# Three small unread transfers ahead of SyncE's first loads in a sparse-attention and spectral-mix kernel

## The chip, the cores and the metric

The kernel runs on one core of one Trainium2 chip. The metric is the device time of one execution in microseconds (us), as the median of several runs. Beside it stands one profiled execution, taken by the hardware profiler, whose span runs from its first to its last instruction. All times in the steps below are counted from the start of that span.

## The reference

Two blocks follow each other. The first is attention over 8 batches, 8 heads, 576 positions and a head size of 64; heads 0 to 3 see only the last 32 positions, heads 4 to 7 only positions that are a multiple of 32 away. The second turns the result along the sequence into frequencies, multiplies the lowest 64 modes by complex matrices of 512 x 512, one for each mode, turns it back, adds, and ends in a product with `w_ch`.

```python
def _attn_ref(q, k, v):                      # q, k, v: (8, 8, 576, 64) float32
    scores = scale * np.matmul(q, k.transpose(0, 1, 3, 2))
    rel = pos[:, None] - pos[None, :]
    mask_local = (rel >= 0) & (rel < 32)
    mask_strided = (rel >= 0) & (pos[None, :] % 32 == pos[:, None] % 32)
    scores = np.where(masks, scores, -1000000000.0)   # heads 0-3 local, 4-7 strided
    attn = softmax(scores)
    return np.matmul(attn, v)

def _moe_ref(x, w_r, w_i, w_ch):             # x: (8, 576, 512); w_r, w_i: (64, 512, 512)
    X = np.fft.rfft(x, axis=1)
    Xr, Xi = np.real(X[:, :64]), np.imag(X[:, :64])
    Yr = np.einsum('bmd,mde->bme', Xr, w_r) - np.einsum('bmd,mde->bme', Xi, w_i)
    Yi = np.einsum('bmd,mde->bme', Xr, w_i) + np.einsum('bmd,mde->bme', Xi, w_r)
    u = x + np.fft.irfft(Y, n=576, axis=1)   # Y is Yr + 1j*Yi in the lowest 64 modes
    return u + np.maximum(u @ w_ch, 0.0)
```

Inputs and output are float32. By far the largest inputs are `w_r` and `w_i`, 64 matrices of 1 MB each.

## The kernel before

The order of the work is written out by hand: each engine runs its instructions in the order of the program, and the framework only adds the semaphore waits.

The kernel has four stages. First, strided attention (heads 4 to 7), batch by batch, until about 80 us; the helpers are `str_v`, `str_q`, `str_k` (transposes on TensorE, copies on VectorE and ScalarE), `str_scores` and `str_values`. Second, local attention (heads 0 to 3), batch by batch, mixed with the first of the modes. Third, the rest of the modes: each mode's two matrices come as one tile `wt` and are multiplied at line 597 or 630 as soon as they have landed. Last, the inverse transform, the product with `w_ch`, and the output, from `osb` tiles by SyncE (line 1028, and at the very end line 1031 by SyncE and ScalarE).

Loading goes by three queues. GpSimd issues everything that is converted from float32 to 16 bits on the way: the rows of v, q and k into the tile `ring` (`load_str`, lines 218 to 222, and `load_loc`) and the weights into `wt` (`w_fetch`, lines 182 to 190). In the profile this is queue q0. A row is 2048 elements, so it appears as one packet of 4 KB. GpSimd's transfers use eight semaphores in turn, so each of them waits for the landing of the eighth transfer before it. A weight transfer also waits until the tile that it overwrites has been used.

The constants are 16-bit tables of the program: `cT` (the Fourier table), `cM6`, `cM5` and `cMl` (the masks) and `cI` (the identity that transposes need). `const_load` (line 109) loads them as they are. ScalarE issues `cI`, `cM6` and `cM5` (queue q10), SyncE `cT` and `cMl` (queue q1). Their issues are among the first instructions of these engines.

The start of the program is this, at line 765:

```python
    psum_pools(tp=3, sc=3, av=2)
    load_str(0, 1)                              # GpSimd: v, q, k of batch 0
    const_load(nc.scalar, "cI", "cM6", "cM5")
    load_str(1, 1)                              # GpSimd: v, q, k of batch 1
    const_load(nc.sync, "cT", "cMl")
    strided_tokens()                            # GpSimd: L327, L328, then L329 reads cT
    load_str(2, 2)                              # GpSimd: v, q, k of batches 2 and 3
    w_fetch()
```

For each of v, q and k in this order, `load_str(0, 1)` issues 64 rows of its batch (line 220) and then eight rows of each of two batches (line 222). `strided_tokens` copies `cT` into `PL` in another order, so GpSimd must have `cT` before it issues the loads of batches 2 and 3. TensorE's first work is the transposes of v at line 276 (`str_v`), which need the rows of v and `cI`. After its two constants SyncE issues nothing until the outputs.

Of the kernel before, what the change touches and what calls it, by code (L numbers as in the profile page):

```python
# [10 lines left out]
FP = mybir.dt.float32  # L11
# [45 lines left out]
def kernel(  # L57
# [10 lines left out]
    nc = tc.nc  # L68
    PSUM = bass.MemoryType.PSUM
    ctx.enter_context(tc.manual_schedule())  # L70
    consts = ctx.enter_context(tc.tile_pool(name="consts", bufs=1))
# [6 lines left out]
    def psum_pools(**bufs):  # L78
        pctx.close()
        pss.clear()  # L80
        for n, c in bufs.items():
            pss[n] = pctx.enter_context(
                tc.tile_pool(name="ps_" + n, bufs=c, space=PSUM)
            )
# [22 lines left out]
    def const_load(eng, *which):  # L107
        for n in which:
            eng.dma_start(cs[n][:, 0 : hosts[names.index(n)].shape[1]], drams[n])
# [100 lines left out]
    def load_str(b, nb):  # L210
        for vi in (2, 0, 1):
            n = 3 * (b % 4) + SLOT[vi]
            two = ring[:, n : n + 4 : 3, :]
            src = SRC[vi][b - b % 2 : b - b % 2 + 2, 4:8].rearrange(
                "b h (c r) d -> (h c) b (r d)", r=32
            )
            if nb == 2:
                nc.gpsimd.dma_start(two[0:64], src[0:64])
            else:
                nc.gpsimd.dma_start(ring[0:64, n, :], src[0:64, b % 2])  # L220
            if b % 2 == 0:
                nc.gpsimd.dma_start(two[64:72], src[64:72])
# [539 lines left out]
            )  # L762


    psum_pools(tp=3, sc=3, av=2)
    load_str(0, 1)
    const_load(nc.scalar, "cI", "cM6", "cM5")
    load_str(1, 1)
    const_load(nc.sync, "cT", "cMl")
    strided_tokens()  # L770
# [342 lines left out]
```

## Time and profile before

| | |
|---|---|
| median of 3 runs | 427.93 us (427.37 to 429.17) |
| profiled execution, span | 426.7 us |
| TensorE / VectorE / ScalarE / GpSimd busy | 81% / 55% / 51% / 26% of the span |
| bytes by DMA | 91.62 MB, mean 215 GB/s |
| share of queue q0 (GpSimd) of the 16 DMA engines | 96.2% |
| first DMA issue, on SyncE and on ScalarE | 0.74 us |
| first DMA issue on GpSimd | 1.23 us |
| `cT` / `cMl`, issue to landing | 2.4 / 2.3 us |
| TensorE's first instruction | 7.1 us |
| first output issued | 396.88 us |

The profiled execution's own time is its span; the median of the unprofiled runs is 1.2 us longer. Bytes are counted as they are written: a row that is converted counts 4 KB, though 8 KB are read. The view by windows gives for each stretch the busy time of each engine, the clock that TensorE was granted, and at the end the busy share of the DMA engines (above 1 where packets overlap) and the rate. The DMA view gives the packets that began in the stretch, the megabytes, and the share of 16 engines' time for each queue. Packets of a few bytes close a transfer; they count in the number of packets and hardly in the time. The chain of waits gives the start, the length and the work of each piece.

### The profile page before, as it was taken

How to read it: one execution, taken by the hardware profiler on the slowest of the kernel's cores; microseconds unless marked ns; L12 is line 12 of the kernel's file. 1: busy time of each engine (PE TensorE's matmuls, PEld its weight loads, DVE VectorE, ACT ScalarE, POOL GpSimd, SP SyncE). 2: the span in 40 equal slices, each digit the busy share in tenths (PEclk: the TensorE clock that was granted, in tenths of full speed). 3: DMA queues.
4: the chain of work that ended last, by engine and by line, in shares of the span. 5: the costliest groups of instructions: out<-in, count | busy, mean ns of one | idle time of the engine just before them, and what ended most of it. 6: DMA issues, size and time to landing. Idle time of an engine off the chain costs nothing.

```text
span 426.7 us, 9768 instructions
## 1 busy us (share of the span) xinstructions
PE 346.4 (81%) x4167; PEld 208.2 (49%) x4167; DVE 234.7 (55%) x466; ACT 218.3 (51%) x390; POOL 110.7 (26%) x196
## 2 busy tenths in 40 slices
PE   2977878769999698889768788878788867889993
PEld 2866767554656365566433344435444423445330
DVE  3788778851355154356113246746676354655884
ACT  1687678643656356556642235423442444443872
POOL 8332333322423222222222322222232222210000
PEclk9999899967999689999995889989999979989997
DMA  8999999999999999999999999999999999995698
GB/s 150 210 212 212 213 213 213 211 211 211 214 213 213 213 213 215 212 214 215 210 214 211 213 214 213 210 213 215 212 213 214 213 213 214 214 212 105 244 355 287
DMA packets 30938, 91.62 MB, mean 215 GB/s; under 512 B 4464, under 2 KB 5232, under 8 KB 30896
## 3 DMA queue, kind: packets, MB, share of 16 engines
q0 software_dynamic: 25168, 81.28, 96.2%
q1 hardware_dynamic: 4976, 9.13, 5.9%
q10 hardware_dynamic: 752, 0.61, 0.5%
q8 instruction: 32, 0.52, 0.5%
q14 instruction: 10, 0.08, 0.0%
HBM read 162.83 MB, written 9.44 MB: 404 GB/s over the span
## 4 chain that ended last, share of the span: by engine, by line
DMA 47%; PE 29%; DVE 14%; ACT 5%; issue 3%; DVEq 0%; POOL 0%; ACTq 0%; POOLq 0%
DMA wt<-in_moe_w_i_dram 38%; DMA wt<-in_moe_w_r_dram 7%; PE y L597 5%; DVE xb L241 3%; DVE kz L283 3%; PE p L987 2%; ACT X L251 2%; PE sc L532 2%; PE tp L413 2%; PE sc L459 1%; PE p L1001 1%; PE y L532 1%; PE p L760 1%; DVE yy L752 1%; DVE rec L240 1%
## 5 line engine op out<-in xcount | busy, mean ns | idle before, releaser
L597 PE MATMUL y<-wt,X 128*32 128x512 f16 (+1 forms) x448 | 70.9, 430 | 20.1 <-DMA wt<-in_moe_w_i_dram 20.1
L186 POOL DMA_DIRECT2D wt<-in_moe_w_r_dram x59 | 34.7, 588 | 126.4 <-PE y L597 56.3
L186 POOL DMA_DIRECT2D wt<-in_moe_w_i_dram x60 | 35.4, 590 | 68.3 <-DMA wt<-in_moe_w_i_dram 44.4
L597 PEld LDWEIGHTS <-X 128*32 128x32 f16 (+1 forms) x448 | 28.1, 140 | 39.4 <-DMA wt<-in_moe_w_i_dram 18.6
L727 DVE COPY xo<-tp 128x512 f16<-128x512 f16 x32 | 22.1, 691 | 36.8 <-PE tp L725 36.8
L726 ACT ACTIVATE v<-sc 128x512 f16<-128x512 f32 x32 | 19.1, 597 | 44.2 <-PE sc L717 44.2
L717 PE MATMUL sc<-w_cp,xT 128*128 128x512 f16 x128 | 36.9, 410 | 1.9 <-DVE xT L690 1.9
L489 ACT ACTIVATE PL<-sc 128x480 f16<-128x480 f32 (+1 forms) x48 | 27.0, 578 | 21.3 <-PE sc L475 21.0
L241 DVE TENSOR_TENSOR xb<-av,rec 90x256 f16<-90x256 f32 (+2 forms) x80 | 36.0, 450 | 2.8
L240 DVE RECIPROCAL rec<-av 90x4 f32<-90x4 f32 (+2 forms) x80 | 14.6, 183 | 39.3 <-PE av L504 28.2
L251 ACT ACTIVATE yr<-y 128x512 f16<-128x512 f32 x28 | 16.7, 597 | 36.8 <-PE y L597 35.6
L961 DVE TENSOR_TENSOR xo<-p,xo 128x1024 f16<-128x1024 f32 x16 | 19.6, 1225 | 21.7 <-PE p L760 21.7
L420 DVE COPY qT<-tp 128x576 f16<-128x576 f16 x16 | 11.9, 752 | 34.7 <-PE tp L413 34.7
L251 ACT ACTIVATE v<-p 128x1024 f16<-128x1024 f32 x16 | 16.4, 1023 | 23.1 <-PE p L760 23.1
L378 ACT ACTIVATE PL<-sc 90x360 f16<-90x360 f32 (+1 forms) x48 | 22.7, 490 | 7.0 <-PE sc L371 6.4
L251 ACT ACTIVATE v<-tp 128x640 f16<-128x640 f16 (+1 forms) x24 | 19.0, 807 | 11.8 <-PE tp L447 9.3
L413 PE MATMUL tp<-cI_s,ring 64*64 64x64 f16 x864 | 22.4, 197 | 2.7 <-DVE qT L420 2.4
L459 PE MATMUL sc<-cMl_s,cI_s 128*128 128x480 f16 (+1 forms) x48 | 19.4, 405 | 4.5 <-ACT PL L489 2.9
L276 PE MATMUL tp<-cI_s,ring 72*128 72x72 f16 x256 | 15.4, 207 | 8.7 <-DMA ring<-in_v_dram 7.1
L413 PEld LDWEIGHTS <-ring 64*64 64x64 f16 x864 | 17.5, 110 | 9.4 <-issue 5.4
L251 ACT ACTIVATE kz<-tp 64x360 f16<-64x360 f16 (+1 forms) x32 | 18.9, 592 | 6.2 <-PE tp L413 5.2
L1013 ACT ACTIVATE rl<-p 128x1024 f32<-128x1024 f32 (+1 forms) x19 | 18.4, 979 | 5.7 <-PE p L1001 3.1
(142 smaller groups left out, 737.9 us busy)
## 6 DMA issues: line engine op xcount, KB each, us to landing
wt<-in_moe_w_i_dram POOLq DMA_DIRECT2D x60, 512.0 KB, 18.8
wt<-in_moe_w_r_dram POOLq DMA_DIRECT2D x59, 512.0 KB, 17.7
out_dram<-osb SPq DMA_DIRECT2D x15, 512.0 KB, 3.4
ring<-in_v_dram POOLq DMA_DIRECT2D x8, 288.0 KB, 13.4
ring<-in_q_dram POOLq DMA_DIRECT2D x8, 288.0 KB, 13.6
ring<-in_k_dram POOLq DMA_DIRECT2D x8, 288.0 KB, 13.1
ring<-in_v_dram POOLq DMA_DIRECT2D x3, 512.0 KB, 14.8
ring<-in_q_dram POOLq DMA_DIRECT2D x3, 512.0 KB, 14.8
```

Of the source, the lines that this page charges most:

```text
L186: nc.gpsimd.dma_start(dst, rows)
L241: nc.vector.tensor_tensor(out=dst, in0=val.rearrange("p h (q c) -> p h c q", c=4), in1=rec[0:n, 0:pieces] .to_broadcast((n, pieces, 64)) . ...
L251: nc.scalar.activation(out=out, in_=in_, func=ACTF.Copy)
L378: nc.scalar.activation(out=PS[0:n, ds(POFF[t], 4 * n)], in_=scp[0:n, 0 : 4 * n], func=ACTF.Exp, scale=SCALE,)
L413: nc.tensor.transpose(tp[ds(64 * hp, 64), ds(64 * i, 64)], qn[ds(64 * hp, 64), ds(64 * (9 * g + i), 64)], idn[ds(64 * hp, 64), ds(64 * hp, ...
L459: nc.tensor.matmul(scp[:, 0 : n * times].rearrange("p (h x) -> p h x", h=times), idn, mask_rows("cMl", n, times), start=True, stop=False,)
L489: nc.scalar.activation(out=dst, in_=src, func=ACTF.Exp, scale=SCALE)
L597: nc.tensor.matmul(yp[ds(a, 32), :], Xh[half][pr, c].rearrange("p b r (h m) -> p (b r h) m", h=2)[:, :, mm % 32], wt[pr, XC[c], :], start= ...
L717: nc.tensor.matmul(vp, xT[:, ch], w_chs["cp"][:, ch, :], start=(ch == 0), stop=(ch == 3),)
L726: nc.scalar.activation(out=v0, in_=vp, func=ACTF.Copy)
L727: nc.vector.tensor_copy(out=xo.rearrange("p (h q c) -> p h q c", h=2, c=4), in_=tp[:, 0:512].rearrange("p (h c q) -> p h q c", h=2, c=4),)
L961: nc.vector.tensor_tensor(out=xo, in0=up[:, 0:n], in1=xo, op=AluOp.add)
```

## The change

A tile `seen` of 16 partitions with three rows of 16 float32 values (192 bytes per partition) is added to the pool of constants. A helper `touch` loads into one of its rows a corner of an input: batch 0, head 4, the first 16 positions and the first 16 of the 64 values, so 16 rows of 64 bytes. It is called three times on SyncE: for v, then for q, then for k. Nothing reads `seen`.

```diff
+    seen = consts.tile([16, 3, 16], FP, name="seen")
+
+    def touch(eng, i, src):
+        eng.dma_start(seen[:, i], src[0, 4, 0:16, 0:16])
+
     psum_pools(tp=3, sc=3, av=2)
+    touch(nc.sync, 0, v)
     load_str(0, 1)
     const_load(nc.scalar, "cI", "cM6", "cM5")
+    touch(nc.sync, 1, q)
+    touch(nc.sync, 2, k)
     load_str(1, 1)
     const_load(nc.sync, "cT", "cMl")
     strided_tokens()
```

On SyncE the order is now v's, q's and k's touch, `cT`, `cMl`, and then the outputs. On the other engines the order of the instructions is the same as before. The tile `seen` lies behind the constants, and the tiles that come after it lie 192 bytes further up in each partition.

## The prediction

> **What bounds the kernel now.** I read the page's slices first, because the change acts on the first microseconds only, and the question is whether anything gained or lost there reaches the end.
>
> ```profile
> DMA  8999999999999999999999999999999999995698
> GB/s 150 210 212 212 213 213 213 211 211 211 214 213 213 213 213 215 212 214 215 210 214 211 213 214 213 210 213 215 212 213 214 213 213 214 214 212 105 244 355 287
> q0 software_dynamic: 25168, 81.28, 96.2%
> ```
>
> The DMA engines run full from the second slice to about 384 us, at 210 to 215 GB/s in every slice, and nearly all of it is q0, the queue that GpSimd feeds with rows of v, q, k and the weights. A stage in which the engines never slacken ends when its bytes are through. So the kernel is a stream of fixed volume, then a tail of about 49 us that starts when the last weights have landed. What the start of the stream loses or gains, the end loses or gains. Only the first slice is below the rate (150 GB/s), so I cut it up by windows.
>
> ```profile
> core 0: us, PE busy (x) PEld busy (x) DVE busy (x) ACT busy (x) POOL busy (x), PEclk, DMA share, GB/s
> 0.00:1.70 1.70, 0.00 (x0) 0.00 (x0) 0.64 (x1) 0.00 (x0) 0.68 (x5) 1.00 0.00 0
> 1.70:2.80 1.10, 0.00 (x0) 0.00 (x0) 0.43 (x1) 0.69 (x1) 1.10 (x3) 1.00 0.90 227
> 2.80:4.05 1.25, 0.00 (x0) 0.00 (x0) 0.00 (x0) 0.60 (x1) 1.25 (x3) 1.00 0.86 72
> 4.05:5.06 1.01, 0.00 (x0) 0.00 (x0) 0.00 (x0) 0.00 (x0) 1.01 (x3) 1.00 0.99 178
> 5.06:7.00 1.94, 0.00 (x0) 0.00 (x0) 0.00 (x0) 0.00 (x0) 1.10 (x3) 1.00 1.09 179
> 7.00:9.00 2.00, 1.21 (x19) 1.09 (x20) 1.14 (x7) 0.83 (x2) 2.00 (x6) 1.00 1.04 193
> 9.00:16.00 7.00, 6.56 (x77) 5.88 (x77) 6.12 (x12) 3.50 (x7) 3.85 (x7) 1.00 1.06 211
> ```
>
> The last two columns count: until 1.70 nothing moves, until 2.80 the constants move, and from 2.80 to 4.05 the engines are 0.86 busy yet move 72 GB/s. The DMA view of that stretch, of its later part, and of the next ones shows who holds them:
>
> ```profile
> q0 software_dynamic: 16, 0.07, 77.2%
> ...
> q10 hardware_dynamic: 1, 0.00, 0.2%
> ...
> q0 software_dynamic: 43, 0.17, 90.3%
> ...
> q0 software_dynamic: 131, 0.33, 103.0%
> ...
> q0 software_dynamic: 151, 0.39, 104.0%
> ...
> q0 software_dynamic: 488, 1.48, 106.5%
> ```
>
> The first line is 2.80 to 4.05: 16 rows, one on each engine. The next is 3.10 to 4.05 alone; then 4.05 to 5.06, 5.06 to 7.00, 7.00 to 9.00 and 9.00 to 16.00. At the steady end, 488 packets less the 128 tiny ones that close transfers are 360 rows of 4 KB; 1.065 x 7.00 x 16 engines / 360 = 0.331 us a row. The first 16 rows, all of v, took 0.772 x 1.25 x 16 / 16 = 0.965 us each: 0.63 us more than steady, on every engine. Something at the first read of v makes the engines wait; the touches aim at that. By the same division (less tiny packets) the 42 rows after them are 0.016 us over steady, the 81 rows to 7.00 are 0.064 over, the 94 to 9.00 0.023 over: 0.04, 0.32 and 0.14 us of each engine. All waiting of this kind is 0.63 + 0.04 + 0.32 + 0.14 = 1.13 us.
>
> **The change, part by part.**
>
> *The prize.* From 2.80 to 9.00 the queue moved 16 + 42 + 81 + 94 = 233 rows, 0.954 MB. At 211 GB/s that is 4.52 us and it took 6.20: the stream is 1.68 us late. Of this 0.32 us is the constants' own transfers on q1 and q10 after 2.80 (6.5% and 2.7% of 1.25 us, 9.1% of 1.01, 5.8% of 1.94). So 1.36 us is the most that warm first reads can give back to the stream, about 0.3% of the kernel; above 1.13 us it is idleness, not waiting.
>
> *The touches' own transfers.* 16 rows of 64 bytes and a closing packet on each engine, three times: 96 packets. The ACT queue's small packets took 19.1% of 1.10 us x 16 for 202, so 0.017 us each; 96 x 0.017 / 16 = 0.10 us.
>
> *The touches' place.* SyncE issues cT at 0.74, and its packets appear with the first DMA work at about 1.70. The touch of v takes that place, 1.1 us before v's first rows at 2.80. So it is early enough: it meets the first wait instead of the rows. The wait itself does not vanish. Its length is between the mean excess of 0.63 us and what the whole stretch allows, 1.25 less one steady row, 0.92 us. It then runs from 1.70 to 2.33 or 2.62.
>
> *What it displaces.* That time was not idle: the constants fill 0.90 of 1.70 to 2.80, 0.99 us of every engine. If they must wait behind the touch, they run after it and push into the rows. The row for this is the later part of v's wait: from 3.10 to 4.05 the ACT queue moved one packet, though the second cM transfer was issued by 2.1, landed 5.5 us after its issue, and moved 44 and 99 packets on q10 in the two windows that follow. A waiting read held the engine for all queues. So I count the touch's wait as 0.63 to 0.92 us pushed into the stream.
>
> The Trainium skill says otherwise in part ("DMA: Bandwidth & Descriptors", section "Queues, rings and completion order"): each engine goes round the queues that have work, packet by packet, so a queue that waits would not stop another. The row of 3.10 to 4.05 disagrees, with one packet in 0.95 us. By the rule the constants would pass and the sum would be -1.26 us; by the row it is the sum below.
>
> *The touches of q and k.* They follow 0.4 us apart. Bound from below: their waits run while that of v runs, 0 us. From above: each holds all engines in turn, 2 x 0.63 to 2 x 0.92 us. Nearest rows: q's and k's first rows cost only 0.32 + 0.14 us in 5.06 to 9.00, and small packets at 0.017 us each are far too short for a whole read, so reads are asked for ahead of their turn. I take 0.2 us, near the lower end.
>
> *The constants of SyncE.* cT and cMl are issued three places later: an issue took 0.36 and 0.42 us, so about 1.2 us. cT landed 2.4 us after its issue, at 3.1. Late by 1.2 and by the touches' wait, 4.4 to 6 us. GpSimd wants it at 7.19 for its copy into PL (line 329), then issues the third pair of loads at 8.29. This is covered by 1 us or more; without cover GpSimd would stall, with the second batch's three loads still queued in front of the engines (16 rows per engine, about 5 us of work), so the stream would not dry up. cI goes by ACT and is needed with v at 7.12. Nothing else waits on SyncE before 396.88.
>
> *Layout.* The tile of 192 bytes moves later tiles up alike; I cost it at nothing, bounded by the run-to-run spread.
>
> Sum, main case: -1.36 + 0.78 (middle of 0.63 and 0.92) + 0.10 + 0.2 = -0.3 us. Bounds: -1.36 + 0.10 = -1.26, if the constants pass the waiting touches and nothing is pushed, and -1.36 + 3 x 0.92 + 0.10 = +1.50. The profiled execution spans 426.7 us and the runs' median is 427.93, so 1.2 us lies around it or is spread. Span 426.4, time 427.6; own range 426.7 to 429.4.
>
> **The rivals.**
>
> *Faster: the start of compute, not the stream, sets the end.* The chain of waits supports it:
>
> ```profile
> 1.23 0.66 POOL ring L220
> 1.88 5.10 DMA ring<-in_v_dram
> 6.98 0.14 issue
> 7.12 0.53 PE tp L276 x6
> ```
>
> It runs through v's landing and then through TensorE, VectorE and ScalarE for some 100 us. If v landed as a constant does (2.4 us) and every later step followed, 2.7 us would go: 425.2. Against it: a buffer freed earlier only lets GpSimd queue a transfer earlier on engines already at 212 GB/s. It needs more than 2.14 us, so nearly the whole shortening of v's landing.
>
> *Slower: the touches pay and the rows pay again.* A first-read wait may belong to the place read, and the rows lie in other places: batch 1 and other heads, while a touch reads 4 KB of batch 0, head 4. Then three waits are held in turn by all engines and nothing is spared: 3 x 0.92 + 0.10 = 2.86 us, 430.8. It decides by more than 0.5% if each touch holds the engines for over 0.68 us. Against it: rows 2 to 4 of an engine, far from the first, were within 0.016 us of steady.
>
> *No effect: the wait belongs to the GpSimd queue's first use, not to v.* Then the touches are quick, the rows wait as before, +0.1 us: 428.0. For it: the first 16 rows carry most of the excess, q's and k's far less. Against it: there is excess at q and k at all.
>
> **How the numbers follow.** The main case gets 0.50, no effect 0.13, the faster rival 0.19, the slower 0.18. The first two lie within 0.5% (2.14 us, about what a measurement of this kernel can tell from no change): same 0.63. The range starts at 425.2, the faster rival, and ends at 429.6, the main case's 429.4 and a little spread (three runs reached from 427.37 to 429.17); it leaves out the slower rival, 0.18.
>
> **What would show it.** Right: DMA work still begins near 1.7 with q1; v's first 16 q0 rows near 0.33 us each; the low GB/s found before 2.80; constants on q10 landing late; steady rate reached within 1 us of before; the last weights near 377. The copy at line 329 should wait for nothing. The faster rival shows as TensorE's first transpose about 2.7 us earlier and last weights earlier by as much. The slower one shows as q0 rows still near 0.96 us and PE's start later than 9. I am wrong altogether if the span moves by over 1.5 us with the steady rate reached when it was before.

## The result and the profile after

The change makes the kernel slower: 429.12 us in the median (427.49 to 430.88) for 427.94 before, a ratio of 1.0027 with a 95% interval of [1.0019, 1.0035]. That is a loss of 1.2 us, between 0.8 and 1.5. One of the 22 runs of before took 459.45 us, far above the others, and is left out of the ratio as a slow one. The time stays within 0.5% and within the predicted range, but it moved beyond its interval the other way than the forecast of 427.6.

The two profiled spans, 426.5 us after and 426.7 before, do not show this. The runs that list both numbers are nearly all 1.8 us longer than their spans (428.28 us for the profiled run after, with 426.5), so the profiled run before stood near 428.5, above its median, and the one after is 0.8 us below its own. What the two traces do show is the start. First the page's line of rates after:

```profile
GB/s 141 209 213 214 212 212 214 210 211 211 212 214 212 214 213 213 214 214 212 213 213 211 213 213 214 212 214 214 212 210 214 213 214 214 213 213 120 246 355 286
```

The plateau is as before, and the first slice carries 141 GB/s for 150: over a slice of 10.67 us that is 96 KB less, or 0.45 us of the stream. The view by windows after, with four of the stretches of before, shows where (last two columns: busy share of the DMA engines, GB/s):

```profile
1.70:2.80 1.10, 0.00 (x0) 0.00 (x0) 0.44 (x1) 0.67 (x1) 1.10 (x3) 1.00 0.74 101
2.80:4.05 1.25, 0.00 (x0) 0.00 (x0) 0.00 (x0) 0.61 (x1) 1.25 (x3) 1.00 0.82 145
4.05:5.06 1.01, 0.00 (x0) 0.00 (x0) 0.00 (x0) 0.00 (x0) 1.01 (x3) 1.00 0.99 207
5.06:7.00 1.94, 0.52 (x10) 0.55 (x11) 0.00 (x0) 0.00 (x0) 1.62 (x6) 1.00 0.92 137
```

From 1.70 to 2.80 the engines moved 227 GB/s before and now 101. From 2.80 to 4.05 the stream looks better than before (145 for 72 GB/s). But then, from 5.06 to 7.00, it drops to 137 GB/s for 179. The timeline of SyncE after, and the DMA issues after (size, microseconds from issue to landing):

```profile
0.74 0.40 SPq L768 DMA_DIRECT2D seen<-in_v_dram  x1
1.20 0.41 SPq L768 DMA_DIRECT2D seen<-in_q_dram  x1
1.66 0.45 SPq L768 DMA_DIRECT2D seen<-in_k_dram  x1
2.14 0.42 SPq L109 DMA_DIRECT2D cT_s<-cT  x1
2.61 0.43 SPq L109 DMA_DIRECT2D cMl_s<-cMl  x1
```

```profile
cT_s<-cT SPq DMA_DIRECT2D x1, 144.0 KB, 4.5
...
cMl_s<-cMl SPq DMA_DIRECT2D x1, 64.0 KB, 7.8
...
seen<-in_v_dram SPq DMA_DIRECT2D x1, 1.0 KB, 1.8
seen<-in_q_dram SPq DMA_DIRECT2D x1, 1.0 KB, 2.1
seen<-in_k_dram SPq DMA_DIRECT2D x1, 1.0 KB, 4.1
```

The touches of v and q land at 2.54 and 3.30. cT is issued 1.4 us later than before and lands at 6.64 instead of 3.1; cMl lands at 10.4 instead of 3.5. The DMA view after shows the exchange, first from 1.70 to 2.80, then from 5.06 to 7.00:

```profile
q0 software_dynamic: 12, 0.05, 43.6%
q10 hardware_dynamic: 282, 0.06, 26.5%
q1 hardware_dynamic: 62, 0.00, 3.5%
...
q0 software_dynamic: 54, 0.19, 73.6%
q1 hardware_dynamic: 95, 0.08, 17.9%
```

Before 2.80 the constants and touches on q1 and q10 now take 30.0% of 1.10 us, 0.33 us of every engine, where the constants took 0.99: so 0.66 us of transfers has left the stretch ahead of the rows. A part of the freed time is used, since twelve rows of v now begin before 2.80, but the constants come back among the rows: in the second stretch q0 moved 0.19 MB for 0.33 before. These are q's rows. TensorE's first work on q before, and then the chain of waits after, show what that does to it:

```profile
8.91 0.64 PE L260 MATMUL tp<-cI_s,ring 72*128 72x72 f16 x8 [0.68 <-DMA ring<-in_q_dram]
```

```profile
3.01 7.19 DMA ring<-in_q_dram
...
10.33 0.65 PE tp L260 x8
```

TensorE starts on v at 6.48, earlier than the 7.12 of before, but gets q only at 10.33 (8.91 before), and VectorE's first reciprocal comes at 18.90 for 17.48.

### The profile page after: what moved, and what is told of

It reads as the page before. It is cut to its first block, busy times and chain, and to the rows that moved or that the text cites. A ratio compares the mean times of both kernels' runs of the same rounds, so it can differ in the third digit from the quotient of the medians.

```text
span 426.5 us, 9774 instructions
## 1 busy us (share of the span) xinstructions
PE 342.9 (80%) x4167; PEld 207.5 (49%) x4167; DVE 235.0 (55%) x466; ACT 218.5 (51%) x390; POOL 111.2 (26%) x196
## 4 chain that ended last, share of the span: by engine, by line
DMA 55%; PE 23%; DVE 12%; ACT 5%; issue 3%; POOL 1%; DVEq 0%; POOLq 0%; ACTq 0%
DMA wt<-in_moe_w_i_dram 40%; DMA wt<-in_moe_w_r_dram 9%; DMA ring<-in_v_dram 4%; PE y L597 4%; DVE xb L241 3%; DVE kz L283 2%; PE p L995 2%; PE sc L532 2%; DMA ring<-in_q_dram 2%; ACT X L251 2%; PE p L1009 1%; DVE yy L752 1%; DVE rec L240 1%; PE av L392 1%; PE sc L717 1%
## 5 line engine op out<-in xcount | busy, mean ns | idle before, releaser
L597 PE MATMUL y<-wt,X 128*32 128x512 f16 (+1 forms) x448 | 68.2, 416 | 22.6 <-DMA wt<-in_moe_w_i_dram 22.6
L186 POOL DMA_DIRECT2D wt<-in_moe_w_r_dram x59 | 34.8, 590 | 121.1 <-PE y L597 40.2
L251 ACT ACTIVATE v<-p 128x1024 f16<-128x1024 f32 x16 | 16.4, 1024 | 19.7 <-PE p L760 19.7
```

The source lines that it names most:

```text
L186: nc.gpsimd.dma_start(dst, rows)
L251: nc.scalar.activation(out=out, in_=in_, func=ACTF.Copy)
L597: nc.tensor.matmul(yp[ds(a, 32), :], Xh[half][pr, c].rearrange("p b r (h m) -> p (b r h) m", h=2)[:, :, mm % 32], wt[pr, XC[c], :], start= ...
```

## The experiments

Three theories stood against each other: displaced constants (A), the first reads of v, q and k (B), and the layout (C). The first four kernels undo or isolate one part each. The measured ratios are against runs of the kernel before on the same chip, whose median was 427.90, and losses in microseconds are taken from the ratio. Edits that keep the tile or the touches of v, q and k are shown against the changed kernel, the others against the kernel before.

**Layout only.** The tile stays, the transfers go.

```diff
-    def touch(eng, i, src):
-        eng.dma_start(seen[:, i], src[0, 4, 0:16, 0:16])
+    nc.vector.memset(seen, 0.0)
...
-    touch(nc.sync, 0, v)
...
-    touch(nc.sync, 1, q)
-    touch(nc.sync, 2, k)
```

> The tile of 192 bytes is kept, so every later tile lies where it does after the change, but no transfer is made: one VectorE memset fills the tile while VectorE waits for v. Three theories for the 1.2 us that the change costs. A, displaced constants: the touches take SyncE's first places, cT and cMl come 1.4 us later and their 0.7 us of engine time falls among the rows instead of into the idle time before 2.8 us. B, first reads: reading a little of v, q and k holds the engines. C, layout: the shift of the later tiles by 192 bytes. A and B expect the time of before, 427.9 (within 0.4); C expects 429.1.

Measured: 427.98 us, ratio 1.0003 [0.9991, 1.0015]. The shift of 192 bytes costs nothing that can be measured, and the interval, up to 0.6 us, leaves out the loss of 1.2; C falls.

**The touches behind the constants.**

```diff
-    touch(nc.sync, 0, v)
...
-    touch(nc.sync, 1, q)
-    touch(nc.sync, 2, k)
...
     const_load(nc.sync, "cT", "cMl")
+    touch(nc.sync, 0, v)
+    touch(nc.sync, 1, q)
+    touch(nc.sync, 2, k)
```

> The three touches stay on SyncE but come after cT and cMl, which so have their old issue times of 0.74 and 1.16. A (displaced constants) expects the loss gone: 427.9, within 0.4, with q0's megabytes by 9 us as before. B (first reads) and C (layout) expect it kept, 429.1: the touches' reads then fall among the rows.

Measured: 428.12 us, ratio 1.0009 [1.0001, 1.0018], 0.4 us. Most of the loss goes when only the order on SyncE is put back. The small rest is above the 0.10 us that the prediction gave the touches' own packets, but its interval begins at 0.04 us.

**The same three transfers from a constant.**

```diff
+    seen = consts.tile([16, 3, 32], F16, name="seen")
...
+        eng.dma_start(seen[:, i], src[0:16, 0:32])
...
+    touch(nc.sync, 0, drams["cI"])
...
+    touch(nc.sync, 1, drams["cI"])
+    touch(nc.sync, 2, drams["cI"])
```

> The three small transfers stay in SyncE's first places with the same 16 rows of 64 bytes, but they read the program's own table cI, which is loaded anyway, and not v, q and k. A (displaced constants) expects the loss of 1.2 us as it is, 429.1, with cT landing near 6.6 and cMl near 10 as after the change. B (first reads) expects it gone, 427.9. If the touches save the rows of v some waiting, A expects slightly more than 429.1, by up to 0.3.

Measured: 428.78 us, ratio 1.0023 [1.0011, 1.0035]. That is 1.0 us: the loss is there though v, q and k are not touched. B falls.

**Late constants, no touch.**

```diff
-    const_load(nc.scalar, "cI", "cM6", "cM5")
+    const_load(nc.scalar, "cI", "cM6", "cM5", "cT", "cMl")
     load_str(1, 1)
-    const_load(nc.sync, "cT", "cMl")
```

> No touch and no tile: cT and cMl are issued by ScalarE behind its own three constants, so at about 2.1 and 2.5 us instead of 0.74 and 1.16, as late as the touches make them. A (displaced constants) expects most of the loss without any touch: 428.6 to 429.1. B and C expect the time of before, 427.9, within 0.3.

Measured: 428.57 us, ratio 1.0031 [1.0012, 1.0051]. Issuing the two constants late, on ScalarE's queue and with no touch, costs 0.7 us by the medians and 1.3 by the ratio, which two long runs (430.70 and 433.36) pull up, which is about what the change costs. The trace is that of the longest run, 433.36. The DMA view from 1.70 to 12.00 puts these kernels in two groups; the line of q0 shows packets, megabytes and share. Before, layout only, and touches last:

```profile
q0 software_dynamic: 560, 1.59, 89.0%
```

```profile
q0 software_dynamic: 570, 1.61, 88.6%
```

```profile
q0 software_dynamic: 566, 1.61, 90.0%
```

After, transfers from a constant, and late constants:

```profile
q0 software_dynamic: 529, 1.49, 83.6%
```

```profile
q0 software_dynamic: 527, 1.49, 84.7%
```

```profile
q0 software_dynamic: 544, 1.52, 84.3%
```

By 12 us the stream is 0.07 to 0.12 MB behind in the second group, which at 212 GB/s is 0.3 to 0.6 us.

**How does it reach the end: stream or compute?** The displaced constants do two things: the stream falls behind, and q lands 1.4 us late. The next kernels part them; the runs of before had a median of 427.74 there. First compute alone is made late, by repeating VectorE's first clearing.

```diff
-    nc.vector.memset(kzs[0], 0.0)
+    for _ in range(8):
+        nc.vector.memset(kzs[0], 0.0)
```

> No touch; the transfers are those of before, in the same order. VectorE clears its first tile eight times instead of once (1.07 us each), so its first copy of v starts near 9.7 instead of 7.67 and the whole start of compute is about 2 us late, which is more than the 1.4 us by which q's landing is late after the change. Two theories of how the displaced constants reach the end. A1, stream: they push the volume of the rows and weights, 0.7 us of engine time; A2, compute: they make q land later and with it every step of compute. A1 expects the time of before, 427.9, within 0.4. A2 expects 429.3 to 429.9.

Measured: 429.99 us, ratio 1.0052 [1.0034, 1.0071], just above what A2 expects. But the dose was larger than planned: each clearing was followed by 0.32 us of idleness, and the first reciprocal came at 22.24, 4.8 us late. So the same with six clearings was run, beside runs of before with a median of 427.71; the first reciprocal is at 19.45, 2.0 us late, more than the 1.4 us of the change.

> As the kernel with eight clearings of VectorE's first tile, but with six, which end near 9.1: VectorE's first copy is about 1.4 us late, as much as the change makes the first reciprocal late (18.90 for 17.48), with no transfer moved. Theory A1 (stream): the loss of the change is the stream's lag, and this kernel takes the time of before, 427.8, within 0.4. Theory A2 (compute): a start of compute that is 1.4 us late costs most of the change's 1.2 us by itself, 428.5 to 429.2, through modes that free their weight tiles too late near 100 to 120 us.

Measured: 427.75 us, ratio 0.9997 [0.9987, 1.0007]. A start of compute that is later than the change makes it shows no cost by itself; 0.3 us is the most that the interval allows. A2 in its simple form falls. The view by windows from 96 to 120 us, before, after, with six and with eight clearings, shows where the larger dose bites (last column GB/s):

```profile
96.00:120.00 24.00, 23.20 (x298) 13.06 (x296) 7.50 (x16) 12.10 (x24) 8.18 (x15) 0.89 1.09 213
```

```profile
96.00:120.00 24.00, 22.79 (x270) 12.85 (x269) 5.94 (x14) 11.66 (x24) 8.44 (x15) 0.86 1.09 212
```

```profile
96.00:120.00 24.00, 22.48 (x254) 12.53 (x255) 5.69 (x12) 11.67 (x25) 8.09 (x15) 0.83 1.08 208
```

```profile
96.00:120.00 24.00, 21.65 (x222) 12.31 (x219) 5.88 (x13) 11.87 (x24) 6.20 (x12) 0.79 0.98 187
```

With eight clearings the stream runs at 187 GB/s here: (213 - 187) x 24 us is 0.62 MB or 2.9 us; the profiled run, 430.86 us, is 3.1 above the median of before. The first modes come too late to free weight tiles: in this stretch GpSimd waited 16.4 us for the products at line 597 before it could issue weights, for 11.4 before. With six clearings the rate is 208 and the wait 13.5 us, the beginning of the same, though the time does not show it. After the change the stretch is at 212, nearly as before.

**The stream alone.** The constants are moved twice: once as before, once more among the rows, into a tile that is idle.

```diff
     const_load(nc.sync, "cT", "cMl")
+    spare = xb[7].rearrange("p a b -> p (a b)")
+    nc.sync.dma_start(spare[:, 0:576], drams["cT"])
+    nc.sync.dma_start(spare[:, 576:832], drams["cMl"])
```

> No touch; cT and cMl are loaded as before and then once more by SyncE into a tile that is idle for the first 60 us, so that 208 KB of constants (0.7 us of every engine by the rows of before) move among the rows while the first copy lands on time and nothing waits for the second. A1 (stream) expects the loss of the change without its lateness: 428.6, and up to 429.1 if the mixing of queues costs more than the engine time. A2 (compute waits for late constants or q) expects less, below 428.4, as far as q lands on time.

Measured: 428.15 us, ratio 1.0010 [1.0000, 1.0020]. That is 0.4 us, less than the 0.7 us of engine time and less than the change's 1.2; A1's 428.6 was not reached, and below 428.4 is what A2 expected. At 12 us q0 was 0.05 MB behind the kernel before (1.54 MB for 1.59). Here q's transposes also started late, at 10.26.

**Both together**, the second copy and six clearings, beside runs of before with a median of 427.80.

> The two single disturbances together and still no touch: cT and cMl moved a second time among the rows (alone +0.4 us), and compute started about 1.4 us late by six clearings on VectorE (alone -0.1 us). If the two simply add, 428.0 to 428.2. If a late stream and a late start of compute together cost more than each alone, because the first modes near 100 us then have no slack left, 428.6 to 429.1, which would account for the part of the change's loss that exceeds the engine time of the constants.

Measured: 428.63 us, ratio 1.0017 [1.0008, 1.0025], 0.7 us. The two alone add to 0.3. It points to an interaction, but the intervals overlap; this does not settle it. In its trace the stretch from 96 to 120 us ran at 213 GB/s, so it does not show the interaction there.

**Parts of the displacement.** With the touch of v alone in front (cT and cMl one place later):

> Only the touch of v stays in front; cT and cMl are one place (0.45 us) later than before instead of three. Displaced constants expects a part of the loss: cT still moves before v's first rows at 2.6 to 2.8, cMl in part behind them, 0.2 to 0.6 us, so 428.1 to 428.5. If the reads of q and k cost by themselves, it expects 427.9.

Measured: 428.02 us, ratio 1.0009 [1.0000, 1.0017], 0.4 us by the ratio, with a median just under the range expected. With the three touches between cT and cMl:

```diff
-    touch(nc.sync, 0, v)
...
+    const_load(nc.sync, "cT")
+    touch(nc.sync, 0, v)
     touch(nc.sync, 1, q)
     touch(nc.sync, 2, k)
...
-    const_load(nc.sync, "cT", "cMl")
+    const_load(nc.sync, "cMl")
```

> SyncE's order is cT, the three touches, cMl. Of the displaced constants only cMl is left, 64 KB of the 208 KB, which nothing needs before some 90 us. Displaced constants expects about a third of the loss by engine time, 0.2 to 0.5 us: 428.0 to 428.3, with q landing within 0.7 us of before. If the touches cost by coming before any rows, it expects 428.6 or more.

Measured: 428.06 us, ratio 1.0006 [0.9993, 1.0019]. Both times are near what a third of the displacement would cost, though the second cannot be told from no loss, and its q was late all the same (transposes at 10.92, for 10.33 after the change). The traces do not follow the times. From 1.70 to 12.00 the kernel with the touch of v alone moved 1.66 MB on q0, more than before, and the one with cT first moved as little as the changed kernel:

```profile
q0 software_dynamic: 528, 1.49, 86.2%
```

So how far the stream is behind at 12 us does not alone decide the loss: this kernel shows the changed kernel's lag with 0.3 us of loss, and its interval reaches from -0.3 to 0.8.

**The change again**, for a second profile.

> The changed kernel itself, beside the same runs of before, for a second profile: the first one is 0.8 us below the median of its runs. Expected 428.9 to 429.3. A1 expects the stream behind by 0.4 to 1.2 us from 16 us on and no further loss; A2 expects in a slow run an additional loss of rate between 96 and 120 us, below 211 GB/s.

Measured: 428.67 us for 427.71, ratio 1.0020 [1.0009, 1.0032]: 0.9 us, a little below the range expected and in agreement with 1.2. The first slice carried 139 GB/s, q0 had moved 1.46 MB by 12 us, and 96 to 120 us ran at 213.

**Can a touch spare the rows at all?** A single run, with the touches reading the very rows of batch 0:

```diff
+    seen = consts.tile([64, 3, 16], FP, name="seen")
...
+        rows = src[0, 4:8].rearrange("h (c r) d -> (h c) (r d)", r=32)
+        eng.dma_start(seen[:, i], rows[0:64, 0:16])
```

> The touches read the first 64 bytes of each of the 64 rows of v, q and k that batch 0 loads first, instead of 4 KB of the first row alone. It tells whether a first read can be taken from the rows at all. If the rows' waits belong to the places read, the first 64 rows of v, q and k should show no time above 0.33 us each, where v's first 16 took 0.60 after the change. If the waits come from the start of the queue and from other queues' packets on the same engine, the first rows stay near 0.6 us and q's keep their excess. The time is 429 or more in both cases, since the constants are displaced further.

Measured: 429.24 us in one run. The DMA view over the first rows of v: after from 2.50 to 3.10, transfers from a constant from 2.50 to 3.33, late constants from 2.50 to 3.20, touched rows from 2.50 to 3.15:

```profile
q0 software_dynamic: 16, 0.07, 99.8%
```

```profile
q0 software_dynamic: 16, 0.07, 69.9%
```

```profile
q0 software_dynamic: 16, 0.07, 88.4%
```

```profile
q0 software_dynamic: 17, 0.07, 89.3%
```

Share times length gives 0.60, 0.58, 0.62 and (over 17 rows) 0.55 us a row. The first rows of v take the same with touches of v, with touches of a constant, with no touch, and with touches of the same rows. They had taken 0.965 us before. That figure is not a fixed price of the constants in front either: in the seven kernels whose first constants go out as before, the same 16 rows took between 0.48 us (the second copy) and 1.12 (touches last), one trace each. That the constants' going out of the way shortened them is likely and not shown; no read ahead is seen to spare them anything.

## Why the prediction was right or wrong

**The prize: the step that failed.** The failed step is the term of -1.36 us. The prediction said that "1.36 us is the most that warm first reads can give back to the stream" and then entered all of it in the sum of the main case. Nothing of it came through a touch. The wait was read as belonging to the first read of v because it lay on v's first rows. The controls show that the 0.37 us gained there, 0.965 less 0.60, appears without any touch of v, and that the same rows can take 0.48 with the constants in place and no touch. Further back the gain was lost again: q0 moved 0.19 MB from 5.06 to 7.00 instead of 0.33. What the runs show in place of the prize is a loss, 1.0 us with touches of a constant and 0.7 to 1.3 with late constants and no touch. Without the prize the sum is 0.78 + 0.10 + 0.2, or +1.1 us, close to the measured 1.2; but that is luck, since two of its terms were reasoned otherwise than the runs show.

**What the touches displace.** The size was right, 0.63 to 0.92 us predicted and 0.66 measured as what left the time before 2.80, and the way was wrong. The engines were not held by a waiting touch: from 1.70 to 2.80 they were busy 0.74 of the time, and q10's 282 packets passed. cT was late because SyncE issued it late, three issues of 0.40 to 0.45 us, and then came behind rows. The row from 3.10 to 4.05, with one packet of q10, was read as a waiting read that holds the engines. After the change the same stretch has two packets of q1, with cT queued, while q0 moved 40 rows at 0.36 us each, near the steady 0.33. So rows in steady motion kept the constants out as well.

The rule of the Trainium skill that the prediction weighed, "DMA: Bandwidth & Descriptors", section "Queues, rings and completion order", has engines go round the queues packet by packet, where a packet is typically 9 to 17 descriptors, so it need not be one packet of the profile. The prediction took the row of 3.10 to 4.05 to contradict it; with such packets it need not. The touch of k and cT still landed 4.1 and 4.5 us after their issue, beside 2.3 to 2.4 us for the same queue's constants before. So the turns gave small packets little while v's rows were queued; how many rows make one turn no run here tells.

**The constants of SyncE.** The issue was predicted 1.2 us later and was 1.4. The landing of cT was put at 4.4 to 6 us and came at 6.64, so the cover of 1 us was gone: GpSimd's copy began at 6.74, just behind. It did not wait for it, as predicted. That q would be the one to land late was not foreseen.

**q's and k's touches, layout.** No wait of 0.2 us shows at a touch; q1's 62 packets before 2.80 took 3.5% of 1.10 us on 16 engines, 0.01 us each. The layout at nothing was right (1.0003).

**The bound.** That the end follows the stream, and not the start of compute, held: 2.0 us late cost nothing that shows. It holds only so far, since 4.8 us late cost 2.2 us, by holding up the stream near 100 us. One reading was off. The tail is not 49 us, and the last weights do not land near 377: that is only TensorE's last wait for weights in the chain before. The last weights land near 391.9, before and after. The chain of waits after shows it:

```profile
382.38 9.57 DMA wt<-in_moe_w_i_dram
```

From that landing to the end of the span it is about 34.6 us after and 34.8 before. It is about 34.6 as well with eight clearings (landing at 394.52, span 429.1) and in the longest trace, late constants (397.03, span 431.6): so the end moved with the landing of the last weights.

**The rivals.** The faster one, compute's start, falls with the six clearings, and TensorE did start on v sooner (6.48 for 7.12) without a gain. The slower one had the sign, but not by its mechanism: no cost of reading the inputs shows, as the loss is there with touches of a constant and with none. The rival of no effect was right that the rows' waits are not v's, and left out what the touches push aside.

**Where the numbers stood.** The prediction tied its span to the median by 1.2 us. The runs' own gap is 1.8, so the trace it was built on was a slower run by some 0.6 us. The chance of 0.63 for within 0.5% fits the outcome, but neither of the two cases that it was added from came about as described.

**What stays open.** That the displaced constants cause the loss is shown: it is there with late constants and no touch, and most of it is gone with the touches behind the constants. Its size is not fully accounted for: the stream is behind by about 0.45 us at 12 us, the second copy of the constants cost 0.4, and the change cost 0.9 to 1.2; with cT first the same lag cost 0.3. The rest may come from stream and compute being late together near 100 us; that is only pointed to. The trace of late constants is for it (201 GB/s from 96 to 120 us, for 213 before). The trace of transfers from a constant, 429.37 us, is against it: the stretch ran at 213, but q0's lag grew from 0.10 MB at 12 us to 0.22 MB at 30 us (5.13 MB for 5.35), which is 1.0 us, in the first attention stage. Why, no run tells.

## What to carry to other kernels

The time before the first large transfer can move is worth as much as any other when the transfer engines bound the kernel: what fills it (here most of 208 KB of constants) is nearly free, and what pushes it out is paid for, even if it is only three transfers of 1 KB. A warm-up read needs a control that costs the same and warms nothing; one such run shows here that the loss comes without the reads, and the touches behind the constants show that most of it lies in the order on SyncE. And for an effect of 0.3%, look at where the profiled run stands among its runs before building a sum on it.

## What had not been expected of the hardware

With the constants late, the first 16 rows of GpSimd's queue took 0.55 to 0.62 us each for a steady 0.33, whether or not their data had been read before; with the constants in front it was 0.48 to 1.12, from kernel to kernel. And 2.0 us of lateness at the start of compute did not show in the time, while 4.8 us cost 2.2: the slack before the first modes ends somewhere between.
